# Sparse attention and a soft mixture of experts on one core: the order of all engine queues planned anew, with other prices

## The chip, the cores and the metric

The kernel runs on one core of one Trainium2 chip. The core has five engines that work side by side and each take their instructions in the order in which they were written: the matrix engine (PE in the profile, its weight loads PEld), VectorE (DVE), ScalarE (ACT), GpSimd (POOL) and SyncE (SP, which here only starts transfers). The metric is the device time of one execution in microseconds; the median of several executions is given.

## The reference

Eight batches of eight heads, 576 positions, head size 64. Attention keeps only those scores that lie within tau (0.02) of the row's largest. Its output, 4608 rows of 512, goes through a soft mixture of eight experts with four slots each.

```python
scores = scale * np.matmul(q, k.transpose(0, 1, 3, 2))
thresh = np.max(scores, axis=-1, keepdims=True) - tau
scores = np.where(scores >= thresh, scores, -1000000000.0)
attn = np.exp(scores - np.max(scores, axis=-1, keepdims=True))
attn = attn / (np.sum(attn, axis=-1, keepdims=True) + 1e-09)
x = np.matmul(attn, v)            # then laid out as (4608, 512)

logits = x @ phi                  # (4608, 32)
d = softmax of logits over the rows, c = softmax over the 32 slots
slot_input = d.T @ x
h = np.maximum(slot_input[e] @ w1[e], 0.0)     # for each expert e
slot_out[e] = h @ w2[e]
out = c @ slot_out
```

All is float32.

## The kernel before

Two heads of one batch make a pair; there are 32 pairs. A pair's 2 x 576 rows of scores are cut into nine blocks of 128 rows, eight of one head each and the ninth (the remainder) of both. For a block i:

- PE computes the scores (qk, L504; L509 for the ninth) into one of four regions of PSUM, each of two banks.
- DVE takes the largest of each row. In blocks 0, 2, 4, 6 and 8 it is a plain reduction (L522, nmx) and the scores stay in PSUM. In blocks 1, 3, 5 and 7 (the list AWAY) one instruction copies the negated scores to SBUF and takes the extreme on the way (L518, ss), so that the region is free at once.
- ACT computes the exponentials (L531, p, or pL for the ninth block). POOL makes the threshold from the maximum (L534, thr, one column).
- DVE compares the scores with the threshold, zeroes what lies below and sums the row, in one instruction (L538). In the AWAY blocks both its tensor inputs, ss and p, are in SBUF; in the others one is in PSUM.

After each second block POOL adds 1e-9 to the sums (L545, ri), DVE takes reciprocals (L548), POOL multiplies the two blocks by them (L552, p times ri, 128 x 576 each), PE transposes the scaled blocks (L429, ptr) and ACT copies them back to SBUF (L434, pTa, pTb, pTl). When all nine are there, PE multiplies by the values (L599), ACT copies the result (xT), PE transposes it again and ACT stores it (x). POOL also scales each pair's keys by 1/8 (L484). SP loads keys, queries and values (L477, L482, L489), two buffers of each.

After each fourth pair (one batch) the function dispatch adds the router's logits and the running sums of the dispatch softmax. Behind the last pair come the experts and the combination (from L894 on); that tail is written by hand and isn't planned. Its weights are loaded during attention, into buffers and into space that attention has given back.

The order of everything up to the tail comes from a planner, the class Order. Functions such as pair and dispatch hand each step to Order.add with an engine, a duration in ns, a nominal place, and the buffers that it reads and writes. Order.plan then plays the program through: whenever an engine is free, it takes from its ready steps the one with the lowest nominal place whose buffers are free. A step becomes ready when those before it have ended and a latency has passed: SAME for a step behind another of its own engine, LAT for one behind another engine's. The starts that come out sort the instructions into the engines' queues. On the chip each engine then follows its queue and waits where an input isn't there.

The nominal place of a step is its pair's base (nine steps a pair) plus a number of the table TABLE. There are tables for the first pair, the last, those between ("pair", 90 numbers, used by pairs 1 to 30), for the dispatch of an even, an odd and the last batch, and for the softmax over the slots ("soft"). A lower number goes first.

Buffers that set what can run ahead: four PSUM regions, four buffers p2 for two blocks of exponentials each, four of nmx and of thr, two of ss (SLOTS).

Of the kernel before, what the change touches and what calls it, by code (L numbers as in the profile page):

```python
# [17 lines left out]
LAT = {"PE": 197, "DVE": 140, "ACT": 152, "POOL": 160, "SP": 4500}  # L18
# [18 lines left out]
for _n, _v in (  # L37
    ("first", [
# [7 lines left out]
    ]),  # L46
    ("pair", [
# [7 lines left out]
    ]),  # L55
    ("last", [
# [7 lines left out]
    ]),  # L64
    ("even", [
        11.70, 6.26, 20.27, 11.43, 9.24, 4.36, 12.47, 23.16, 21.02, 7.45, 12.14, -0.83, -28.24, 0.76,
        8.10, -112.07, -111.39, 12.77, 9.31, 51.37, 18.87,
    ]),
    ("odd", [
        15.17, 39.73, 8.52, 14.62, 8.10, 2.55, 9.85, 14.30, 12.02, -15.66, 1.70, 14.42, 66.80, -1.30,  # L70
        10.34, 27.16, 5.02, -5.68, 21.85, 41.74, 36.19, -19.82, -3.87,
    ]),
    ("end", [
# [3 lines left out]
    ]),  # L77
    ("soft", [
        26.07, 93.95, 64.32, 18.60, -8.26, 26.88,
    ]),  # L80
):
    TABLE.update({(_n, _i): _x for _i, _x in enumerate(_v) if _x is not None})
# [19 lines left out]
class Order:  # L102
# [3 lines left out]
    def __init__(self, slots):  # L106
        self.slots = {k: list(v) for k, v in slots.items()}
        self.ops = []
        self.noms = []
        self.seen = set()  # L110
        self.newest = {}
        self.where = ["", 0, 0]
        self.writers = {}
        self.readers = {}
# [14 lines left out]
    def add(self, eng, dur, nom, fn, r=(), w=(), after=(), mode=HALVES):  # L129
        i = len(self.ops)  # L130
        name, base, n = self.where
        self.where[2] += 1
        self.noms.append((name, n, base, nom - base))
        r = [self.key(x) for x in r]
        w = [self.key(x) for x in w]
        deps = set(after)
        for x in r:
            deps.update(self.hits(self.writers, x))
        for x in w:
            deps.update(self.hits(self.writers, x))  # L140
            deps.update(self.hits(self.readers, x))
        for x in r:
            self.readers.setdefault(x[0], {}).setdefault(x[1], []).append(i)
        for x in w:
            self.writers.setdefault(x[0], {}).setdefault(x[1], []).append(i)
        bufs = {id(x[0]): x[0] for x in r + w}.values()
        for x in bufs:
            if x not in self.seen:
                self.seen.add(x)
                self.newest[x.kind] = i  # L150
        self.ops.append((eng, dur, fn, sorted(deps), list(bufs), mode))

    def plan(self, table):
# [46 lines left out]
        mode = None  # L200
        ev = [(0.0, 1, i) for i in range(n) if left[i] == 0]
        heapq.heapify(ev)
        while ev:
# [10 lines left out]
            for eng in engs:  # L214
# [21 lines left out]
                end = t + o[1]  # L236
                if eng == "PE":
                    end += SWITCH * (o[5] != mode)
                    mode = o[5]
                engfree[eng] = end  # L240
                heapq.heappush(ev, (end, 2, -1))
                heapq.heappush(ev, (end + LAT[eng], 0, got))
                for j in succ[got]:
                    left[j] -= 1
                    lat = (SAME if ops[j][0] == eng else LAT)[eng]
# [25 lines left out]
def softmax_attention_soft_moe(  # L271
# [170 lines left out]
    def dve(dur, nom, r, w, fn):  # L442
        G.add("DVE", dur, nom, fn, r, w)
# [13 lines left out]
    def pair(p):  # L457
# [38 lines left out]
        for i in range(N9):  # L496
# [4 lines left out]
            def qk(i=i, c=c, h=h, s=s):  # L501
                for g in range(2):
# [9 lines left out]
            G.add("PE", 540 if i < 8 else 486, t + OFF['qk'], qk, [kt[h], qt[h, 0], qt[h, 1]] if i < 8 else [kt, qt], [s],  # L512
                  mode=HALVES if i < 8 else QUADS)
            away = i in AWAY
            ss = Buf("ss") if away else s
            if away:

                dve(729, t + OFF['mx'], [s], [ss, nmx], lambda s=s, ss=ss, nmx=nmx: nc.vector.tensor_scalar(  # L518
# [8 lines left out]
            else:  # L527
# [3 lines left out]
            G.add("ACT", 624, t + OFF['ex'], lambda sv=sv, nmx=nmx, view=view, away=away: nc.scalar.activation(  # L531
# [5 lines left out]
            dve(950 if away else 729, t + OFF['st'], [ss, thr], [dst, r[i]],  # L537
                lambda sv=sv, thr=thr, view=view, i=i, away=away: nc.vector.scalar_tensor_tensor(  # L538
# [4 lines left out]
            if h == 1 or i == 8:  # L543
                e = slice(i // 2 * 2, i + 1)
                pool(200, t + OFF['ri'], lambda e=e: nc.gpsimd.tensor_scalar(  # L545
# [523 lines left out]
```

## Time and profile before

| | us |
|---|---|
| median of 3 runs | 597.59 |
| lowest and highest | 593.55 and 598.43 |
| span of the profiled execution | 595.4 |

The profile is of one execution. Its pages give busy time by engine, busy time by stretch, groups of instructions by line (count, busy us, mean ns of one, idle time of the engine just before them and who ended it), who waited for whom, and the instructions in order of time. A busy PE isn't PE at its peak, since matmuls overlap and their ends are modelled. An engine's idle time counts only where that engine bounds the work.

### The profile page before, as it was taken

To read this page: it belongs to the slowest core of one execution; us is meant where nothing else is said; L and a number is where in the kernel's file an instruction comes from. 1 tells how busy PE (TensorE), PEld (TensorE's weight loads), DVE (VectorE), ACT (ScalarE), POOL (GpSimd) and SP (SyncE) were. 2 spreads that over 40 slices of the span, in tenths; PEclk is the share of its full clock that TensorE was granted. 3 is DMA by queue.
4 is the path that set the end of the run, shared out by engine and by line. 5 is a ranking of instruction groups with operands and counts; after the bars stand their busy time and mean duration, and the time that the engine had idled before them with its cause. 6 is when DMAs were issued, how large, how long until landed. Compare 5 with 4: busy or idle time off the path is not lost. (4 is left out here: it accounts for less than half of the span.)

```text
span 595.4 us, 17443 instructions
## 1 busy us (share of the span) xinstructions
PE 548.3 (92%) x6404; PEld 340.6 (57%) x6404; DVE 496.8 (83%) x1275; ACT 448.2 (75%) x753; POOL 410.8 (69%) x799
## 2 busy tenths in 40 slices
PE   8799999999999999999999999999999899799991
PEld 6465665555665565566666655556666465453471
DVE  5889998999999989999999999999999889231183
ACT  3588887988888888888888978898888778422071
POOL 2778886888878887888788868887888666411030
PEclk9699999999999999999999999999999989899996
DMA  6245554455445555333333333333333312799678
GB/s 167 61 94 148 160 154 137 138 147 155 129 133 158 150 154 149 83 84 84 83 85 83 85 83 83 84 83 84 84 83 84 83 32 67 245 367 407 253 306 328
DMA packets 31988, 82.97 MB, mean 139 GB/s; under 512 B 4640, under 2 KB 12832, under 8 KB 31904
## 3 DMA queue, kind: packets, MB, share of 16 engines
q1 hardware_dynamic: 31904, 81.87, 46.8%
q8 instruction: 50, 0.82, 0.6%
q14 instruction: 34, 0.28, 0.2%
HBM read 72.42 MB, written 9.44 MB: 137 GB/s over the span
## 5 line engine op out<-in xcount | busy, mean ns | idle before, releaser
L552 POOL TENSOR_SCALAR p<-p,ri 128x576 f32<-128x576 f32 x256 | 206.8, 815 | 27.2 <-DVE ri L548 11.3
L504 PE MATMUL ps<-k,q 64*128 64x288 f32 x1024 | 170.1, 437 | 16.8 <-DVE ss L518 11.3
L429 PEld LDWEIGHTS ps<-ident,p 64*128 64x128 f32 x2304 | 92.2, 140 | 59.8 <-POOL p L552 17.8
L538 DVE SCALAR_TENSOR_TENSOR p<-ss,thr,p 128x576 f32<-128x576 f32 x128 | 116.9, 915 | 4.4 <-POOL thr L534 2.9
L522 DVE TENSOR_REDUCE nmx<-ps 128x1 f32<-128x576 f32 x160 | 116.8, 752 | 4.3 <-PE ps L504 2.9
L429 PE MATMUL ps<-ident,p 64*128 64x64 f32 x2304 | 108.9, 228 | 10.0 <-POOL p L552 6.1
L504 PEld LDWEIGHTS ps<-k,q 64*128 64x128 f32 x1024 | 85.9, 190 | 51.0 <-DVE ss L518 18.7
L538 DVE SCALAR_TENSOR_TENSOR p<-ps,thr,p 128x576 f32<-128x576 f32 x128 | 101.9, 811 | 8.9 <-POOL thr L534 7.3
L531 ACT ACTIVATE p<-ss,nmx 128x576 f32<-128x576 f32 x128 | 96.7, 776 | 12.8 <-DVE ss L518 12.4
L518 DVE TENSOR_SCALAR_CACHE_REDUCE ss<-ps 128x576 f32<-128x576 f32 x128 | 96.0, 750 | 6.7 <-PE ps L504 5.4
L434 ACT COPY pTb<-ps 128x1024 f32<-128x1024 f32 (+1 forms) x95 | 82.1, 874 | 21.0 <-PE ps L429 19.2
L531 ACT ACTIVATE p<-ps,nmx 128x576 f32<-128x576 f32 x128 | 91.9, 739 | 6.4 <-DVE nmx L522 3.9
L534 POOL TENSOR_SCALAR thr<-nmx,nabs 128x1 f32<-128x1 f32 x160 | 70.6, 445 | 11.2 <-DVE nmx L522 6.3
L599 PE MATMUL ps<-pTb,vv 128*64 128x320 f32 x512 | 76.0, 439 | 1.9 <-ACT pTb L434 1.7
L434 ACT COPY pTa<-ps 128x1024 f32<-128x1024 f32 x64 | 64.8, 1012 | 11.5 <-PE ps L429 8.6
L545 POOL TENSOR_SCALAR ri<-r 128x2 f32<-128x2 f32 (+1 forms) x160 | 38.9, 243 | 48.4 <-DVE p L538 21.0
L599 PE MATMUL ps<-pTa,vv 128*64 128x256 f32 x512 | 65.5, 400 | 0.0
L599 PEld LDWEIGHTS ps<-pTb,vv 128*64 128x64 f32 x512 | 33.9, 136 | 30.7 <-ACT pTl L434 2.2
L534 POOL TENSOR_SCALAR thr<-nmx,pabs 128x1 f32<-128x1 f32 x128 | 36.6, 286 | 15.8 <-DVE ss L518 10.9
L599 PEld LDWEIGHTS ps<-pTa,vv 128*64 128x64 f32 x512 | 35.2, 142 | 18.1 <-issue 2.2
L599 PE MATMUL ps<-pTl,vv 128*64 128x256 f32 (+1 forms) x256 | 41.9, 406 | 0.0
L859 POOL TENSOR_TENSOR c<-lall,crow 128x512 f32<-128x512 f32 x9 | 9.3, 1043 | 43.9 <-PE ct L421 38.9
(133 smaller groups left out, 605.4 us busy)
## 6 DMA issues: line engine op xcount, KB each, us to landing
w<-in_w SPq DMA_DIRECT2D x44, 512.0 KB, 6.7
q<-in_qT SPq DMA_DIRECT2D x62, 288.0 KB, 4.6
vv<-in_vt SPq DMA_DIRECT2D x32, 320.0 KB, 3.1
host<-in_w SPq DMA_DIRECT2D x20, 512.0 KB, 6.1
k<-in_kT SPq DMA_DIRECT2D x62, 144.0 KB, 4.9
out<-w SPq DMA_DIRECT2D x8, 512.0 KB, 3.3
out<-host SPq DMA_DIRECT2D x8, 512.0 KB, 5.0
out<-host SPq DMA_DIRECT2D x4, 256.0 KB, 4.4
```

Source lines behind the costliest of these rows:

```text
L429: nc.tensor.transpose(out=s[:, g, c:c + 64], in_=ins[g], identity=ident[rows[g], rows[g]], tile_position=(64 * g, 0))
L434: G.add("ACT", 51 + 0.833 * n, nom, lambda: nc.scalar.copy(*io()), r, w)
L504: nc.tensor.matmul(s.t[:, g, 0:HS], qt.t[rows[g], h, c * 128:(c + 1) * 128], kt.t[rows[g], h * HS:(h + 1) * HS], start=True, stop=True, ti ...
L518: dve(729, t + OFF['mx'], [s], [ss, nmx], lambda s=s, ss=ss, nmx=nmx: nc.vector.tensor_scalar(out=ss.t.rearrange("p (a k) -> p a k", a=2), ...
L522: dve(665, t + OFF['mx'], [s], [nmx], lambda s=s, nmx=nmx: nc.vector.tensor_reduce(out=nmx.t, in_=s.t[:, :, 0:HS], axis=AX.XY, op=ALU.max, ...
L531: G.add("ACT", 624, t + OFF['ex'], lambda sv=sv, nmx=nmx, view=view, away=away: nc.scalar.activation(view().rearrange("p (a k) -> p a k", ...
L534: pool(250, t + OFF['th'], lambda nmx=nmx, thr=thr, away=away: nc.gpsimd.tensor_scalar(out=thr.t, in0=nmx.t, scalar1=1.0 if away else -1.0 ...
L538: lambda sv=sv, thr=thr, view=view, i=i, away=away: nc.vector.scalar_tensor_tensor(out=view().rearrange("p (a k) -> p a k", a=2), in0=sv() ...
L545: pool(200, t + OFF['ri'], lambda e=e: nc.gpsimd.tensor_scalar(out=ri.t[:, e], in0=r.t[:, e], scalar1=1e-9, scalar2=1.0, op0=ALU.add, op1= ...
L552: pool(725, t + OFF['sc'], lambda k=k, view=view_: nc.gpsimd.tensor_scalar(out=view(), in0=view(), scalar1=ri.t[:, k:k + 1], **one), [ri[c ...
L599: nc.tensor.matmul(lone(w)[h * 64:(h + 1) * 64, 0:n], vv.t[:, v0:v0 + 64], p0, start=(kb == 0), stop=(kb == 4), tile_position=(0, h * 64), ...
L859: nc.gpsimd.tensor_tensor(out=c4, in0=lall[:, rows].unsqueeze(2).to_broadcast([128, k, 4, NS]), in1=crow[:, rows].unsqueeze(2).unsqueeze(3 ...
```

## The change

No step is added or taken out. Three things change in the planner and its inputs.

First, its prices. LAT is changed, and a new table CROSS gives a latency for seven pairs of engines. Several durations are changed: scores, the copy of the AWAY blocks, the exponential, the threshold sums, and the small step before the reciprocal. Scores get another 120 ns of latency (more=120). A PE step that starts after PE has been idle costs 50 ns more.

Second, a rule for DVE and POOL. The threshold sums of the AWAY blocks carry port=True. Where POOL is still at work when such a sum starts, the sum is made longer by 0.4 of what is left of POOL's step; and a POOL step that starts while such a sum runs is made longer by what is left of the sum.

Third, all seven tables are replaced. In "pair", the numbers of DVE's steps go from between -55 and +81 to between -365 and -206, those of ACT from between -76 and +30 to between -197 and -106. POOL's thresholds go from between -48 and +62 to between -124 and -59, its scalings of blocks 0, 1 and 8 from +31, +21 and +15 to +121, +122 and +122, the other scalings from between -34 and +42 to between -92 and -44. PE's go from between -74 and +12 to between -7 and +17. For SP the keys go from -3.06 to +10.31, the queries from -29.12 and -61.01 to +21.95 and +20.10, the values from +30.02 to +25.05. In "even" and "odd" many numbers go from between -112 and +67 to several hundred below zero, the lowest to -1092.31. Steps of other kinds (weight loads, warm-up) keep their places.

```diff
-LAT = {"PE": 197, "DVE": 140, "ACT": 152, "POOL": 160, "SP": 4500}
+LAT = {"PE": 252, "DVE": 150, "ACT": 165, "POOL": 86, "SP": 4500}
+CROSS = {("PE", "DVE"): 260, ("DVE", "ACT"): 182, ("DVE", "POOL"): 220, ("ACT", "DVE"): 237, ("ACT", "POOL"): 250,
+         ("POOL", "DVE"): 61, ("POOL", "ACT"): 100}
 SAME = {"PE": 0, "DVE": 127, "ACT": 143, "POOL": 0, "SP": 2100}
...
     ("even", [
-        11.70, 6.26, 20.27, 11.43, 9.24, 4.36, 12.47, 23.16, 21.02, 7.45, 12.14, -0.83, -28.24, 0.76,
-        8.10, -112.07, -111.39, 12.77, 9.31, 51.37, 18.87,
+        20.61, 146.84, 13.21, 163.00, 29.27, 166.25, 11.28, -584.76, -641.03, -307.50, 19.64, -567.09, -633.13, 123.48,
+        -13.49, -641.02, 163.01, -9.38, -650.04, -12.77, -683.63,
     ]),
...
-    def add(self, eng, dur, nom, fn, r=(), w=(), after=(), mode=HALVES):
+    def skip(self, n):
+        self.where[2] += n
+
+    def add(self, eng, dur, nom, fn, r=(), w=(), after=(), mode=HALVES, more=0, port=False, own=None):
...
-        self.ops.append((eng, dur, fn, sorted(deps), list(bufs), mode))
+        self.ops.append((eng, dur, fn, sorted(deps), list(bufs), mode, more, port))
...
                 end = t + o[1]
+                if o[7]:
+                    end += 0.4 * max(0.0, min(engfree["POOL"] - t, o[1]))
+                    held = end
+                if eng == "POOL" and held > t:
+                    end += held - t
                 if eng == "PE":
-                    end += SWITCH * (o[5] != mode)
+                    end += SWITCH * (o[5] != mode) + 50 * (engfree[eng] < t)
                     mode = o[5]
                 engfree[eng] = end
                 heapq.heappush(ev, (end, 2, -1))
-                heapq.heappush(ev, (end + LAT[eng], 0, got))
+                heapq.heappush(ev, (end + LAT[eng] + o[6], 0, got))
                 for j in succ[got]:
                     left[j] -= 1
-                    lat = (SAME if ops[j][0] == eng else LAT)[eng]
+                    lat = SAME[eng] if ops[j][0] == eng else CROSS.get((eng, ops[j][0]), LAT[eng]) + o[6]
...
-            G.add("PE", 540 if i < 8 else 486, t + OFF['qk'], qk, [kt[h], qt[h, 0], qt[h, 1]] if i < 8 else [kt, qt], [s],
-                  mode=HALVES if i < 8 else QUADS)
+            G.add("PE", 488 if i < 8 else 500, t + OFF['qk'], qk, [kt[h], qt[h, 0], qt[h, 1]] if i < 8 else [kt, qt], [s],
+                  mode=HALVES if i < 8 else QUADS, more=120)
...
-                dve(729, t + OFF['mx'], [s], [ss, nmx], lambda s=s, ss=ss, nmx=nmx: nc.vector.tensor_scalar(
+                dve(674, t + OFF['mx'], [s], [ss, nmx], lambda s=s, ss=ss, nmx=nmx: nc.vector.tensor_scalar(
...
-            G.add("ACT", 624, t + OFF['ex'], lambda sv=sv, nmx=nmx, view=view, away=away: nc.scalar.activation(
+            G.add("ACT", 668 if away else 630, t + OFF['ex'], lambda sv=sv, nmx=nmx, view=view, away=away: nc.scalar.activation(
...
-            dve(950 if away else 729, t + OFF['st'], [ss, thr], [dst, r[i]],
-                lambda sv=sv, thr=thr, view=view, i=i, away=away: nc.vector.scalar_tensor_tensor(
+            G.add("DVE", 738, t + OFF['st'], port=away, r=[ss, thr], w=[dst, r[i]],
+                fn=lambda sv=sv, thr=thr, view=view, i=i, away=away: nc.vector.scalar_tensor_tensor(
...
-                pool(200, t + OFF['ri'], lambda e=e: nc.gpsimd.tensor_scalar(
+                pool(292, t + OFF['ri'], lambda e=e: nc.gpsimd.tensor_scalar(
```

More of the change, by code (lines that the diff above doesn't have):

```diff
@@ L38 @@
     ("first", [
[7 rows of a table removed]
[7 rows of a table added]
     ]),
     ("pair", [
[7 rows of a table removed]
[7 rows of a table added]
     ]),
     ("last", [
[7 rows of a table removed]
[7 rows of a table added]
     ]),
     ("even", [
-        11.70, 6.26, 20.27, 11.43, 9.24, 4.36, 12.47, 23.16, 21.02, 7.45, 12.14, -0.83, -28.24, 0.76,
-        8.10, -112.07, -111.39, 12.77, 9.31, 51.37, 18.87,
+        20.61, 146.84, 13.21, 163.00, 29.27, 166.25, 11.28, -584.76, -641.03, -307.50, 19.64, -567.09, -633.13, 123.48,
+        -13.49, -641.02, 163.01, -9.38, -650.04, -12.77, -683.63,
     ]),
     ("odd", [
-        15.17, 39.73, 8.52, 14.62, 8.10, 2.55, 9.85, 14.30, 12.02, -15.66, 1.70, 14.42, 66.80, -1.30,
-        10.34, 27.16, 5.02, -5.68, 21.85, 41.74, 36.19, -19.82, -3.87,
+        16.01, -65.21, 13.21, -81.20, 26.13, -98.85, 7.02, -280.60, -256.65, -1092.31, 18.10, -183.06, -214.95, -85.79,
+        -4.28, -274.17, -81.33, -258.17, -63.02, 23.32, -252.02, -7.84, -187.13,
     ]),
     ("end", [
[3 rows of a table removed]
[3 rows of a table added]
     ]),
     ("soft", [
-        26.07, 93.95, 64.32, 18.60, -8.26, 26.88,
+        6.88, 35.49, -71.51, 6.87, 39.48, 49.38,
     ]),
@@ L112, in __init__ @@
         self.where = ["", 0, 0]
+        self.own = {}
         self.writers = {}
@@ L127, in scope @@
         self.where = [name, base, 0]
-    def add(self, eng, dur, nom, fn, r=(), w=(), after=(), mode=HALVES):
+    def skip(self, n):
+        self.where[2] += n
+    def add(self, eng, dur, nom, fn, r=(), w=(), after=(), mode=HALVES, more=0, port=False, own=None):
         i = len(self.ops)
-        name, base, n = self.where
-        self.where[2] += 1
+        where = self.where if own is None else self.own.setdefault((own, self.where[1]), [own, self.where[1], 0])
+        name, base, n = where
+        where[2] += 1
         self.noms.append((name, n, base, nom - base))
@@ L200, in plan @@
         mode = None
+        held = 0.0
         ev = [(0.0, 1, i) for i in range(n) if left[i] == 0]
```

48 rows, old and new, of the table TABLE are left out of this document.

## The prediction

> **What bounds the kernel now.** I read the page's busy times first.
>
> ```profile
> span 595.4 us, 17443 instructions
> PE 548.3 (92%) x6404; PEld 340.6 (57%) x6404; DVE 496.8 (83%) x1275; ACT 448.2 (75%) x753; POOL 410.8 (69%) x799
> ```
>
> No engine is full, so I cut the span into stages with the view of busy time by stretch (columns: sum of the stretch, then busy time and count of PE, PEld, DVE, ACT, POOL, granted clock, DMA share, GB/s).
>
> ```profile
> 0.00:30.00 30.00, 24.49 (x162) 16.53 (x162) 20.28 (x58) 13.02 (x18) 15.44 (x44) 0.83 0.48 113
> 30.00:480.00 450.00, 427.99 (x5342) 268.79 (x5340) 421.58 (x1094) 384.60 (x644) 362.60 (x703) 1.00 0.42 111
> 480.00:531.60 51.60, 45.20 (x538) 28.34 (x534) 33.66 (x92) 32.09 (x57) 25.46 (x47) 0.97 0.49 171
> 531.60:595.40 63.80, 50.64 (x373) 26.91 (x372) 21.27 (x33) 18.52 (x34) 7.26 (x7) 0.92 0.84 329
> ```
>
> The change can act on the first 531.6 us; the last 63.8 us are written after the planned part and stay. In the 450 us of steady attention PE is idle 22.0 us and DVE 28.4 us: two engines, each nearly full, take turns in waiting for each other. POOL has 87.4 us to spare there and bounds nothing by itself.
>
> The step from pair to pair comes from one row per pair, the threshold sum of the remainder block, in the view in order of time:
>
> ```profile
> 210.04 0.82 DVE L538 SCALAR_TENSOR_TENSOR pL<-ps,thr,pL 128x576 f32<-128x576 f32 x1
> 318.85 0.82 DVE L538 SCALAR_TENSOR_TENSOR pL<-ps,thr,pL 128x576 f32<-128x576 f32 x1
> 333.51 0.82 DVE L538 SCALAR_TENSOR_TENSOR pL<-ps,thr,pL 128x576 f32<-128x576 f32 x1
> ```
>
> Eight pairs with their two dispatches take 123.47 us, 15.4 us a pair; one pair without a dispatch takes 14.66 us.
>
> Then the groups by line (count, busy us, mean ns, idle time before and what ended it):
>
> ```profile
> L538 DVE SCALAR_TENSOR_TENSOR p<-ss,thr,p 128x576 f32<-128x576 f32 x128 | 116.9, 915 | 4.4 <-POOL thr L534 2.9 <-ACT p L531 1.1
> L538 DVE SCALAR_TENSOR_TENSOR p<-ps,thr,p 128x576 f32<-128x576 f32 x128 | 101.9, 811 | 8.9 <-POOL thr L534 7.3 <-ACT p L531 1.0
> L534 POOL TENSOR_SCALAR thr<-nmx,nabs 128x1 f32<-128x1 f32 x160 | 70.6, 445 | 11.2 <-DVE nmx L522 6.3 <-DVE ri L548 1.4 <-DMA k<-in_kT 0.2
> L534 POOL TENSOR_SCALAR thr<-nmx,pabs 128x1 f32<-128x1 f32 x128 | 36.6, 286 | 15.8 <-DVE ss L518 10.9 <-DVE crow L772 2.4 <-DVE ri L548 1.7
> L552 POOL TENSOR_SCALAR p<-p,ri 128x576 f32<-128x576 f32 x256 | 206.8, 815 | 27.2 <-DVE ri L548 11.3 <-PE ps L509 4.9 <-PE ps L504 3.2
> ```
>
> The same sum over the same 576 columns takes 915 ns with both inputs in SBUF and 811 ns with one in PSUM. The same one-column threshold takes 445 ns in one group and 286 ns in the other. Why, one place in order of time shows:
>
> ```profile
> 123.22 0.74 POOL L484 TENSOR_SCALAR k<-k,flag 128x576 f32<-128x576 f32 x1
> 123.45 1.11 DVE L538 SCALAR_TENSOR_TENSOR p<-ss,thr,p 128x576 f32<-128x576 f32 x1
> 123.94 1.23 POOL L552 TENSOR_SCALAR p<-p,ri 128x576 f32<-128x576 f32 x1
> ```
>
> The sum starts 0.51 us before POOL's key scaling ends and takes 1.11 us, 0.30 more than 811 ns. The next POOL instruction starts inside the sum and takes 1.23 us, where the scaling before it took 0.74. Each holds the other up, and the later one pays. The Trainium skill, page "SBUF — State Buffer", section "Who interferes with whom", says that a DVE instruction with two SBUF inputs contends with a GpSimd instruction that reads SBUF, and that the one issued second fully blocks until the first finishes. Here that would make the sum 0.51 + 0.81 = 1.32 us; the row has 1.11, so most of the instruction is blocked, not all of it.
>
> Last, who waited for whom (us, times, longest):
>
> ```profile
> DVE ri L548 <- POOL ri L545: 8.9, 22, 2.0
> PE ps L504 <- DVE ss L518: 11.3, 20, 1.2
> PEld ps L429 <- POOL p L552: 17.8, 26, 1.4
> PE ps L429 <- POOL p L552: 6.1, 17, 1.1
> POOL k L484 <- DMA k<-in_kT: 3.8, 5, 2.3
> SPq L489 <- PE ps L599: 345.4, 30, 17.6
> ```
>
> **The change part by part.** No instruction is added, removed or resized: 17443 before and after, apart from waits. All that moves is the order in each engine's queue, through the planner's prices and the priority table.
>
> *The prices come nearer to the trace.* Three links, each where the later engine stood waiting:
>
> ```profile
> 222.45 0.74 PE L504 MATMUL ps<-k,q 64*128 64x288 f32 x4
> 223.31 0.76 DVE L522 TENSOR_REDUCE nmx<-ps 128x1 f32<-128x576 f32 x1 [0.24 <-PE ps L504]
> 98.95 1.42 DVE L522 TENSOR_REDUCE nmx<-ps 128x1 f32<-128x576 f32 x2 [0.26 <-PE ps L504]
> 99.81 0.27 POOL L534 TENSOR_SCALAR thr<-nmx,nabs 128x1 f32<-128x1 f32 x1 [0.20 <-DVE nmx L522]
> 153.38 0.76 ACT L531 ACTIVATE p<-ps,nmx 128x576 f32<-128x576 f32 x1
> 154.24 0.82 DVE L538 SCALAR_TENSOR_TENSOR p<-ps,thr,p 128x576 f32<-128x576 f32 x1 [0.32 <-ACT p L531]
> ```
>
> From start to start, scores to maximum is 0.86 us (the old plan reckons 540 + 197 = 0.74, the new one 488 + 120 + 260 = 0.87), maximum to threshold 0.86 (old 665 + 140 = 0.81, new 0.89), exponential to sum 0.86 (old 624 + 152 = 0.78, new 630 + 237 = 0.87). The old plan put work 0.05 to 0.12 us too early at each of these links in every one of nine blocks a pair, and so let other work be queued behind an instruction that was not ready. On the other side it gave a two-SBUF sum a flat 950 ns, while its own row means 915, and nothing to POOL for being held.
>
> *DVE's stretch.* 128 x (915 - 811) = 13.3 us, all on an engine that is idle only 6% of the steady stage. The new plan lets a sum that starts while POOL is at work pay 0.4 of what is left, so a start beside a wide POOL instruction now has a price, though a low one: 0.4 x 0.51 = 0.20 where the row shows 0.30. POOL is busy 81% of the stage, so most sums will still meet it. Between nothing and all, I take half: 6.6 us. By the skill's full block the same place would cost 0.51; a plan that asks 0.20 for it would then be 2.5 times too cheap to keep sums clear of POOL, and with nothing of the stretch recovered the time would be 591.2 us.
>
> *DVE waiting for POOL's small results.* 2.9 + 7.3 us for thresholds and 8.9 us for reciprocals, 19.1 us. A threshold is late where it was held behind a sum or queued behind a scaling of 815 ns. In the new table of a pair the thresholds stand between -124 and -59, most scalings between -92 and -44, and those of blocks 0, 1 and 8 at +121 and +122, so small work more often overtakes wide work. But some of what goes here turns into DVE waiting for PE. I take a third: 6.4 us. Ends: 19.1 gained, or 6.4 lost if the holds fall worse.
>
> *PE's waits for a PSUM region* (11.3 us for scores behind the copy that empties one) depend on DVE getting to that copy. PE's and DVE's waits are two sides of one loop, so I count nothing for them beyond the two terms above. Uncovered it is 11.3 us either way.
>
> *The dispatch of a batch* goes from table values near 0 to values as low as -1092, ahead of everything. It costs DVE the same instructions; what it displaces waits once per batch, eight times at most one 815 ns instruction, 6.5 us, if nothing is queued to cover it; I take 0, since every attention block has neighbours ready.
>
> *The loads on SP.* In the table of a pair, keys go from -3 to +10 and queries from -61 and -29 to +20 and +22, still before the values at +25. Against them the weight loads, with no table, now come first when both are ready. Cover: SP sits 345.4 us waiting for a value buffer, so it is early by far. If the cover goes, the nearest price is POOL's 3.8 us of waiting for keys. I take 0, ends -3.8 and +3.8.
>
> *The last pair and the end of attention* (480 to 531.6): PE is idle 6.4 us there, DVE 17.9. Its tables are drawn anew, with no reason in the rows for a sign: 0, ends -6 and +6.
>
> Sum: 6.6 + 6.4 = 13.0 us, so a span of 582.4. The profiled execution's span is 2.2 us under the 597.59 us median of the runs; with that kept, **584.6 us**, 2.2% faster. A difference over 1% (6 us) is about what a measurement of this kernel can tell from no change.
>
> **The rivals.**
> *Larger gain.* All of stretch and POOL waits goes, 13.3 + 19.1 = 32.4 us. PE's own idle time caps it: 22.0 + 6.4 = 28.4 us, so 597.6 - 28.4 = 569.2. For it: every price moved towards the rows. Against: POOL has to fit 363 us of work beside DVE's sums whatever the order.
>
> *No change.* PE is 95% busy in the steady stage, and what DVE saves comes back as PE waiting for regions and scalings: about 595 to 598. For it: 11.3 us of score blocks waiting for a region, and no buffer is added. Against: the stretch of 13.3 us is real DVE work that a mere shift between waits doesn't restore. The skill's page "Perfetto Trace Analysis", section "Optimization Strategy", says that the same gap repeated on the engine that should be saturated can mean too little SBUF or PSUM for the next tile; by that an order alone would leave these gaps, and the four regions stay four.
>
> *Slower.* The scalings of blocks 0 and 1 go to the very end of POOL's priorities (+121 and +122, from +31 and +21), and the transposes of that pair of blocks need both. PE already waits 17.8 us before weight loads and 6.1 us before matmuls for scalings. One more wide POOL instruction of 815 ns in front in each of 31 pairs, exposed on PE, costs 25.3 us: 597.6 - 13.0 + 25.3 = 609.9. It decides from 16 exposed ones on, every second pair. Against: four buffers for pairs of blocks stand between, and POOL is idle a fifth of the stage.
>
> **How the numbers follow.** Chances: the forecast, from 577 to 591.6, 0.50; larger gain, below 577, 0.12; no change within 1%, 0.23; slower, 0.15. So faster 0.62, same 0.23, slower 0.15. The range may leave out 0.2: it runs from the larger gain's 569 to 602, which leaves out the slower cases (0.15) and the top of "no change", with the losing ends above (6.4, 3.8 and 6 us) set one at a time against half the gain. The forecast's own range is 577 to 592.
>
> **What would show it.** Right: the mean of the two-SBUF sum falls from 915 towards 860, DVE's idle time for thresholds and reciprocals from 19.1 to about 13, the plain step from 14.66 to about 14.2, PE busier than 95% in the stage. Wrong: the stretch stays and POOL's wide instructions are held as before; or DVE's waits shrink while rows of PE waiting for the scalings at L552 or for L518 grow by as much; or keys come late on POOL.

## The result, and the profile after

| | us |
|---|---|
| before, median of 4 runs (593.55 to 598.43) | 596.94 |
| after, median of 4 runs (575.45 to 577.45) | 576.77 |
| ratio, with its 95% interval | 0.968 (0.964 to 0.971) |
| span of the profiled execution, before and after | 595.4 and 574.5 |

The changed kernel is 3.2% faster; 2.2% was forecast, 584.6 us with a range of 569 to 602. The page after (line numbers have moved by 13: L517 is the scores, L531 the copy to ss, L535 the maximum, L547 the threshold, L551 the sums, L558 and L561 the reciprocal's two steps, L565 the scaling):

```profile
span 574.5 us, 17496 instructions
PE 537.0 (93%) x6404; PEld 334.3 (58%) x6404; DVE 489.8 (85%) x1275; ACT 442.2 (77%) x753; POOL 398.1 (69%) x799
```

The same work in the same number of instructions on each engine; only waits were added. Busy time by stretch after the change:

```profile
0.00:30.00 30.00, 24.45 (x216) 17.15 (x216) 21.69 (x63) 15.44 (x24) 16.19 (x47) 0.94 0.47 114
30.00:460.00 430.00, 415.16 (x5258) 261.51 (x5256) 409.70 (x1078) 374.60 (x636) 346.11 (x693) 1.00 0.42 115
460.00:509.10 49.10, 45.78 (x565) 29.25 (x560) 37.17 (x103) 33.64 (x60) 28.41 (x53) 1.00 0.49 172
509.10:574.50 65.40, 51.59 (x372) 26.39 (x372) 21.28 (x33) 18.52 (x34) 7.42 (x8) 0.92 0.84 331
```

PE is now busy 96.5% of the steady stage, from 95.1%, and 93% of the end, from 88%. To say where the time went I cut both kernels at the same events, the remainder sums (pL) of pairs 1 and 29 and the first expert matmul, in the view in order of time, before and then after:

```profile
41.53 0.81 DVE L538 SCALAR_TENSOR_TENSOR pL<-ps,thr,pL 128x576 f32<-128x576 f32 x1
473.76 0.81 DVE L538 SCALAR_TENSOR_TENSOR pL<-ps,thr,pL 128x576 f32<-128x576 f32 x1
531.58 0.64 PE L894 MATMUL h<-w,siT 128*32 128x512 f32 x4
```

```profile
38.08 0.81 DVE L551 SCALAR_TENSOR_TENSOR pL<-ps,thr,pL 128x576 f32<-128x576 f32 x1
293.25 0.81 DVE L551 SCALAR_TENSOR_TENSOR pL<-ps,thr,pL 128x576 f32<-128x576 f32 x1
307.50 0.81 DVE L551 SCALAR_TENSOR_TENSOR pL<-ps,thr,pL 128x576 f32<-128x576 f32 x1
458.90 0.81 DVE L551 SCALAR_TENSOR_TENSOR pL<-ps,thr,pL 128x576 f32<-128x576 f32 x1
509.13 1.05 PE L907 MATMUL h<-w,siT 128*32 128x512 f32 x6
```

| stretch | before | after | gained |
|---|---|---|---|
| start to pair 1 | 41.5 | 38.1 | 3.4 |
| pair 1 to pair 29 | 432.2 | 420.8 | 11.4 |
| pair 29 to the first expert matmul | 57.8 | 50.2 | 7.6 |
| tail | 63.8 | 65.4 | -1.6 |

The step between two pairs without a dispatch falls from 14.66 us to 14.25 (307.50 - 293.25). The groups after:

```profile
L551 DVE SCALAR_TENSOR_TENSOR p<-ss,thr,p 128x576 f32<-128x576 f32 x128 | 110.2, 873 | 1.0
L551 DVE SCALAR_TENSOR_TENSOR p<-ps,thr,p 128x576 f32<-128x576 f32 x128 | 103.8, 812 | 2.5 <-POOL thr L547 0.3 <-issue 0.2
L561 DVE RECIPROCAL ri<-ri 128x2 f32<-128x2 f32 (+1 forms) x160 | 22.9, 156 | 1.0 <-POOL ri L558 0.9
L565 POOL TENSOR_SCALAR p<-p,ri 128x576 f32<-128x576 f32 x256 | 193.9, 762 | 12.0 <-DVE ri L561 3.1 <-PE ps L517 1.2 <-PE ps L442 0.7
```

The sums with both inputs in SBUF fell from 915 to 873 ns and POOL's scalings from 815 to 762. Who waited for whom between pair 1 and pair 29, before and after (us, times, longest):

```profile
DVE p L538 <- POOL thr L534: 9.0, 50, 0.4
DVE ri L548 <- POOL ri L545: 6.2, 19, 0.8
DVE ss L518 <- PE ps L504: 1.9, 6, 0.4
DVE nmx L522 <- PE ps L504: 1.0, 4, 0.3
PE ps L504 <- DVE ss L518: 9.9, 18, 0.6
PE ps L429 <- POOL p L552: 4.0, 15, 0.6
```

```profile
DVE p L551 <- POOL thr L547: 0.3, 1, 0.3
DVE ss L531 <- PE ps L517: 3.5, 13, 0.5
DVE nmx L535 <- PE ps L517: 6.9, 28, 0.3
PE ps L517 <- DVE ss L531: 5.1, 15, 0.3
```

DVE's waiting for POOL, 15.2 us, is all but gone. Its waiting for PE's scores grew from 2.9 to 10.4 us in its place: PE, 96.5% busy, now comes nearest to setting the pace of the steady stage.

Of the 11.4 us between pair 1 and pair 29, 7.4 are in the fifteen steps without a dispatch (221.2 us in all before, 213.8 after) and 4.0 in the thirteen with one (211.0 and 207.0). The gains at the start and at the end hold a part that belongs to the clock (last section).

### The profile page after: what moved, and what is told of

Its sections match the earlier page's. It is cut to its first block, busy times and chain, and to the rows that moved or that the text cites. A ratio compares the mean times of both kernels' runs of the same rounds, so it can differ in the third digit from the quotient of the medians.

```text
span 574.5 us, 17496 instructions
## 1 busy us (share of the span) xinstructions
PE 537.0 (93%) x6404; PEld 334.3 (58%) x6404; DVE 489.8 (85%) x1275; ACT 442.2 (77%) x753; POOL 398.1 (69%) x799
## 4 chain that ended last, share of the span: by engine, by line
PE 54%; DVE 15%; ACT 9%; issue 8%; POOL 8%; DMA 4%; SPq 1%; DVEq 0%; ACTq 0%; POOLq 0%
PE ps L612 23%; PE ps L442 11%; PE ps L517 11%; POOL p L565 4%; DVE p L551 4%; ACT pTb L447 4%; DVE ss L531 3%; DMA host<-in_w 3%; DVE nmx L535 3%; PE ps L522 2%; PE so L941 2%; POOL thr L547 2%; ACT pTl L597 2%; ACT pTl L447 2%; PE h L907 1%
## 5 line engine op out<-in xcount | busy, mean ns | idle before, releaser
L565 POOL TENSOR_SCALAR p<-p,ri 128x576 f32<-128x576 f32 x256 | 193.9, 762 | 12.0 <-DVE ri L561 3.1
L517 PE MATMUL ps<-k,q 64*128 64x288 f32 x1024 | 167.3, 431 | 8.4 <-DVE ss L531 6.5
L535 DVE TENSOR_REDUCE nmx<-ps 128x1 f32<-128x576 f32 x160 | 119.9, 753 | 11.7 <-PE ps L517 7.8
L551 DVE SCALAR_TENSOR_TENSOR p<-ss,thr,p 128x576 f32<-128x576 f32 x128 | 110.2, 873 | 1.0
L517 PEld LDWEIGHTS ps<-k,q 64*128 64x128 f32 x1024 | 85.2, 188 | 38.8 <-DVE ss L531 11.7
L551 DVE SCALAR_TENSOR_TENSOR p<-ps,thr,p 128x576 f32<-128x576 f32 x128 | 103.8, 812 | 2.5 <-POOL thr L547 0.3
L544 ACT ACTIVATE p<-ss,nmx 128x576 f32<-128x576 f32 x128 | 99.4, 781 | 8.2 <-DVE ss L531 8.1
L531 DVE TENSOR_SCALAR_CACHE_REDUCE ss<-ps 128x576 f32<-128x576 f32 x128 | 96.2, 752 | 7.5 <-PE ps L517 6.5
L544 ACT ACTIVATE p<-ps,nmx 128x576 f32<-128x576 f32 x128 | 94.5, 739 | 5.8 <-DVE nmx L535 4.1
L558 POOL TENSOR_SCALAR ri<-r 128x2 f32<-128x2 f32 (+1 forms) x160 | 43.9, 274 | 55.1 <-DVE p L551 36.0
L547 POOL TENSOR_SCALAR thr<-nmx,nabs 128x1 f32<-128x1 f32 x160 | 58.6, 367 | 21.2 <-DVE ri L561 13.4
L612 PE MATMUL ps<-pTa,vv 128*64 128x256 f32 x512 | 62.3, 385 | 0.6 <-DVE ss L531 0.4
L547 POOL TENSOR_SCALAR thr<-nmx,pabs 128x1 f32<-128x1 f32 x128 | 46.8, 366 | 12.3 <-DVE ss L531 8.4
```

The costliest lines, as they stand in the source:

```text
L517: nc.tensor.matmul(s.t[:, g, 0:HS], qt.t[rows[g], h, c * 128:(c + 1) * 128], kt.t[rows[g], h * HS:(h + 1) * HS], start=True, stop=True, ti ...
L531: dve(674, t + OFF['mx'], [s], [ss, nmx], lambda s=s, ss=ss, nmx=nmx: nc.vector.tensor_scalar(out=ss.t.rearrange("p (a k) -> p a k", a=2), ...
L535: dve(665, t + OFF['mx'], [s], [nmx], lambda s=s, nmx=nmx: nc.vector.tensor_reduce(out=nmx.t, in_=s.t[:, :, 0:HS], axis=AX.XY, op=ALU.max, ...
L544: G.add("ACT", 668 if away else 630, t + OFF['ex'], lambda sv=sv, nmx=nmx, view=view, away=away: nc.scalar.activation(view().rearrange("p ...
L547: pool(250, t + OFF['th'], lambda nmx=nmx, thr=thr, away=away: nc.gpsimd.tensor_scalar(out=thr.t, in0=nmx.t, scalar1=1.0 if away else -1.0 ...
L551: fn=lambda sv=sv, thr=thr, view=view, i=i, away=away: nc.vector.scalar_tensor_tensor(out=view().rearrange("p (a k) -> p a k", a=2), in0=sv(),
```

## The experiments

**GpSimd out of the way, in both orders.** If the gain came from how DVE and POOL meet, the old order should win most of it when POOL's scaling costs next to nothing, and the new one little. Two edits, each in both kernels with their queues unchanged: the scaling over one column, or a fill that writes as much and reads nothing. Both leave out the division by the row sums.

```diff
-    out=view(), in0=view(), scalar1=ri.t[:, k:k + 1], **one), [ri[c]], [dst_])
+    out=view()[:, 0:1], in0=view()[:, 0:1], scalar1=ri.t[:, k:k + 1], **one), [ri[c]], [dst_])
```

```diff
-    nc.gpsimd.tensor_scalar(out=view(), in0=view(), scalar1=ri.t[:, k:k + 1], **one)
+    nc.gpsimd.memset(view(), 1.0)
```

> The kernel before, queues unchanged, with GpSimd's scaling of the exponentials cut from 576 columns to 1 (the other 575 stay unscaled, so the attention output is not divided by its row sums). Theory A (the gain of the change comes from how VectorE and GpSimd meet: stretched sums, thresholds and reciprocals that come late): this order loses most of that, 13 to 25 us, and comes to 572 to 584. Theory B (the gain comes from all other prices: work queued behind something that was not ready on PE, ACT and DVE): GpSimd was not what held it, and it gains at most 6 us, 591 to 597.

> The changed kernel with the same cut: GpSimd's scaling over 1 column, the rest unscaled. Theory A: this order had already got rid of most meetings, so it gains less than the kernel before does, 3 to 10 us (567 to 574), and the distance between the two orders falls from 20 us to 12 or less. Theory B: the two gain alike, and the distance stays at 17 us or more.

> The kernel before with GpSimd's scaling replaced by a fill with ones of the same 128 x 576 (the exponentials are overwritten, so the attention weights are all one). GpSimd stays about as busy but reads nothing from SBUF for it. If the stretch of VectorE's two-SBUF sums comes from GpSimd's reads, their mean falls from 915 ns to about 815 and the fill isn't held; theory A with the port alone then gives 8 to 15 us (582 to 589). If GpSimd's being late is what counts, rather than the port, it gains under 4 us.

> The changed kernel with the same fill in place of the scaling. Theory A with the port alone: the sums fall from 873 ns to about 815, and the time by 3 to 8 us (569 to 574), less than in the kernel before. Otherwise the two move alike.

| | old order | new order | distance |
|---|---|---|---|
| as they are (the new one from the first comparison) | 596.6 | 576.8 | 19.8 |
| scaling of one column | 587.5 | 575.8 | 11.7 |
| fill | 588.5 | 576.3 | 12.2 |

The old order gains 9.1 and 8.1 us, the new one 1.0 and 0.5. Neither theory's numbers were met whole. A had asked for 13 us or more from the narrow scaling, B for 6 or less; with the fill the old order met A's 8 to 15, at 588.5, while the new order moved less than the 3 to 8 expected. The distance met A's 12 or less with the narrow scaling. POOL holds 8 of the 20 us, and 12 come from elsewhere. In the steady stage its share is 4 of the 11.4 us: from pair 1 to pair 29 the old order takes 427.7 and 427.9 us with the two edits in place of 432.2, the new one 420.6 and 420.5 in place of 420.8. The 7 us that stay between the orders are about as much in steps with a dispatch (210.8 and 206.9 with the narrow scaling) as in those without (217.0 and 213.7). The group of two-SBUF sums in the new order with the fill:

```profile
L551 DVE SCALAR_TENSOR_TENSOR p<-ss,thr,p 128x576 f32<-128x576 f32 x128 | 103.2, 812 | 5.2 <-ACT p L544 4.3
```

The fill keeps POOL at work on as many columns (577 ns a time, where the scaling took 762) and the sums are down to 812 ns from 873 (in the old order to 830 from 915), so it is POOL's reading that stretches them. (The Trainium skill, page "SBUF — State Buffer", section "Who interferes with whom", says that such a DVE instruction contends with a GpSimd instruction that reads SBUF and not with one that only writes it. The trace agrees.) And in the new order the stretch was harmless where it was left: 60 ns less on each sum changed the time by 1 us at most. The plain step, old order with narrow scaling and then new with it:

```profile
301.05 0.81 DVE L538 SCALAR_TENSOR_TENSOR pL<-ps,thr,pL 128x576 f32<-128x576 f32 x1
315.52 0.81 DVE L538 SCALAR_TENSOR_TENSOR pL<-ps,thr,pL 128x576 f32<-128x576 f32 x1
```

```profile
292.43 0.81 DVE L551 SCALAR_TENSOR_TENSOR pL<-ps,thr,pL 128x576 f32<-128x576 f32 x1
306.69 0.81 DVE L551 SCALAR_TENSOR_TENSOR pL<-ps,thr,pL 128x576 f32<-128x576 f32 x1
```

14.47 us and 14.26: in these rows 0.19 of the 0.41 us that the plain step gained is POOL and 0.22 is not.

**The other half of the step: one group of transposes.** PE's queues of the two orders, read from the traces, differ in a plain step mainly in one place: the transposes of blocks 0 and 1 stand before the previous pair's second product with the values in the old order, and behind that pair's last transposes in the new one. (The queues of DVE, ACT and POOL differ in more places.) What they run into, PE in order of time, old and new:

```profile
303.01 0.65 PE L429 MATMUL ps<-ident,p 64*128 64x64 f32 x16
304.31 1.25 PE L504 MATMUL ps<-k,q 64*128 64x288 f32 x6 [0.64 <-DVE ss L518]
```

```profile
292.35 0.71 PE L442 MATMUL ps<-ident,p 64*128 64x64 f32 x16
293.39 0.76 PE L517 MATMUL ps<-k,q 64*128 64x288 f32 x4 [0.33 <-DVE ss L531]
```

I gave the old plan that one constraint (with the old prices and table), then also the place of the copy that follows, then both with the narrow scaling.

```diff
-    def ptr(n, nom, r, w, triples):
+    def ptr(n, nom, r, w, triples, after=()):
...
-        G.add("PE", 62 * n, nom, fn, r, w)
+        G.add("PE", 62 * n, nom, fn, r, w, after)
...
-                    for h in range(2) for k in range(4)])
+                    for h in range(2) for k in range(4)],
+                    [xtr[-1]] if c == 0 and p % 4 > 1 and 1 < p < NP - 1 else [])
...
         w = Buf("s")
+        xtr.append(len(G.ops))
         ptr(4, u + OFF['x'], [xT], [w, x["t", j]], lambda w=w: [
```

> The kernel before with its prices and table, and one more constraint in its plan: in pairs p with p mod 4 of 2 or 3 the transposes of blocks 0 and 1 come behind the last transposes (x) of pair p - 1, where the changed kernel has them, in place of before that pair's second product with the values. Theory C (with GpSimd out of the way the step without a dispatch still was 14.47 us in the old order and 14.24 in the new; the rest is this move, which fills PE's wait of 0.64 us for a PSUM region): PE's wait before the third block's scores falls to about 0.35 us, and the step between two such pairs from 14.66 to 14.3 to 14.45, 3 to 5 us over all (592 to 594). Theory D (no single move pays; the parts of an order fit each other only as a whole): the step stays at 14.6 or grows, and the time is 596 or more.

Measured 602.7 us, ratio 1.012 (1.007 to 1.016): slower, theory D. The steps between two moved pairs take 14.73 to 15.47 us. PE's wait only moved, one group ahead:

```profile
303.57 0.71 PE L429 MATMUL ps<-ident,p 64*128 64x64 f32 x16 [0.72 <-ACT pTa L434]
```

These transposes wait for ACT's copy of the moved ones, which the old order places behind the remainder block's exponential. So the copy was moved too:

```diff
-                [ss, nmx], [dst])
+                [ss, nmx], [dst], pt0 if i == 8 and p % 4 > 1 and 1 < p < NP - 1 else [])
...
+                if c == 0:
+                    pt0[:] = [len(G.ops)]
                 act_copy(1024, t + OFF['te'], [w], [pT[c]], lambda c=c, w=w, pT=pT: (
```

> The move of the transposes of blocks 0 and 1 again, and with it the copy of their result on ScalarE ahead of the remainder block's exponential of the pair before, where the changed kernel has it (before, PE waited 0.72 us for that copy after the move). If the move failed for want of the copy in its place, the step between two moved pairs falls from 14.78 us with the move alone to 14.3 to 14.5, below the 14.66 of the kernel before, and the whole to 590 to 597; the steps with a dispatch are not planned for it and may stay longer. If the move pays only with the whole new order, that step stays at 14.7 or more.

> The same with GpSimd's scaling cut to 1 column (the rest unscaled). If the 0.42 us between the plain steps of the two orders (14.66 and 14.24) is GpSimd's part of 0.19 and this move's 0.23, nothing else is left and the step between two moved pairs comes to 14.2 to 14.3. If there is a third part it stays above 14.35.

With copy: 599.0 us, ratio 1.005 (1.003 to 1.007), still no gain. The seven steps between two moved pairs take 14.51 to 14.79 us and 14.67 on average, not the 14.3 to 14.5 expected. With the narrow scaling on top: 590.4 us, and the step is 14.29 where it was looked at (mean of the seven 14.39, the first two being longer):

```profile
300.77 0.81 DVE L540 SCALAR_TENSOR_TENSOR pL<-ps,thr,pL 128x576 f32<-128x576 f32 x1
315.06 0.81 DVE L540 SCALAR_TENSOR_TENSOR pL<-ps,thr,pL 128x576 f32<-128x576 f32 x1
```

Five of the seven steps are 14.25 to 14.30, as without a third part; the mean is above 14.35. So transposes and copy in the new places bring this one step of the old order to the new one's, but only with POOL out of the way. That they pay over the stage is not shown: the plain step behind it, into a pair that isn't moved, is 14.68 us where the narrow scaling alone has 14.47, and pair 1 to pair 29 takes 428.1 us against 427.7. With POOL at work they make its meetings worse. The group of sums with move and copy, POOL at full width:

```profile
L540 DVE SCALAR_TENSOR_TENSOR p<-ss,thr,p 128x576 f32<-128x576 f32 x128 | 121.1, 948 | 6.3 <-POOL thr L536 5.1 <-POOL ri L547 0.4 <-ACT p L533 0.3
```

The two halves aren't two independent edits, and no run here has the move and POOL's full work together at a gain. (The 590.4 us, 2.9 more than with the narrow scaling alone, include an end of 56.9 us in place of 53.8.)

**The prices alone.** All new prices and the rule, with the old table (the first lines of the edit, against the changed kernel).

```diff
-    ("first", [
-        -249.67, -228.94, -242.55, 86.26, -279.10, -285.18, -279.09, 21.49, -260.83, -14.00, 73.55, -89.27, -23.01, 140.75,
+    ("first", [
+        -91.66, -86.70, -91.31, -101.39, -117.22, -95.99, -92.60, -93.20, -71.14, -98.63, -93.39, -82.51, -117.60, -89.54,
...
```

> All new prices, with the rule for GpSimd, but the old table. If prices near the trace are what pays by themselves: 580 to 592. If table and prices are only worth something together, since the table's numbers were found for other prices: no gain or a loss, 597 to 630.

606.4 us, ratio 1.018 (1.014 to 1.022), slower. The meetings are there as before (906 ns for a two-SBUF sum), and DVE waits more for thresholds and exponentials:

```profile
DVE p L551 <- POOL thr L547: 12.4, 31, 0.9
DVE p L551 <- ACT p L544: 12.0, 25, 0.8
```

A price doesn't order anything by itself; a planner that takes the ready step of lowest number avoids a costly start only if the numbers were found under that price. The reverse, the new table under the old prices, was not run.

**The tables of the edges.** The old kernel with the new tables last, end and soft; and the new kernel with the old tables first, last, end and soft. The diffs exchange those lists and nothing else, such as

```diff
     ("soft", [
-        26.07, 93.95, 64.32, 18.60, -8.26, 26.88,
+        6.88, 35.49, -71.51, 6.87, 39.48, 49.38,
     ]),
```

in the first and the other way in the second.

> The kernel before with the tables last, end and soft of the changed kernel; pairs 0 to 30 keep their order nearly to the end. From the remainder sum of pair 29 to the first expert matmul the kernel before takes 57.8 us and the changed one 50.2. If the new tables of the end carry this by themselves: 51 to 54 us, and 4 to 6 us less in all (591 to 593). If they need the new prices and the new middle: 57 or more, 596 to 602.

> The changed kernel with the old tables first, last, end and soft. The steady stage should keep its step of 14.24 us. If start and end are worth what the two traces differ there (3.4 and 7.6 us): 584 to 590. If the tables of the edges matter little beside the prices: 577 to 580.

The first: 594.4 us, ratio 0.997 (0.995 to 0.999), and from pair 29's sum to the first expert matmul 54.6 us in place of 57.8 (527.71 - 473.09):

```profile
473.09 0.81 DVE L538 SCALAR_TENSOR_TENSOR pL<-ps,thr,pL 128x576 f32<-128x576 f32 x1
527.71 0.64 PE L894 MATMUL h<-w,siT 128*32 128x512 f32 x4
```

That is 3.2 of the 7.6 us, just short of what was expected if the tables carried it. The second: 596.3 us, ratio 1.000 (0.998 to 1.003), worse than the 584 to 590 expected. Its steady steps are the new kernel's, but the start and the end lose all that these win: the remainder sums of pairs 1 and 2 are 21.1 us apart, and the end takes 58.7 us (526.59 - 467.88).

```profile
35.03 0.82 DVE L551 SCALAR_TENSOR_TENSOR pL<-ps,thr,pL 128x576 f32<-128x576 f32 x1
56.14 0.81 DVE L551 SCALAR_TENSOR_TENSOR pL<-ps,thr,pL 128x576 f32<-128x576 f32 x1
467.88 0.81 DVE L551 SCALAR_TENSOR_TENSOR pL<-ps,thr,pL 128x576 f32<-128x576 f32 x1
526.59 0.64 PE L907 MATMUL h<-w,siT 128*32 128x512 f32 x4
```

**The rule for GpSimd.** Two tables found by the same random search, from the old table on, with the new prices and as many trials: one with the rule, one without it. All seven tables are other numbers in each, and in the second the rule is off:

```diff
-                if o[7]:
+                if False:
                     end += 0.4 * max(0.0, min(engfree["POOL"] - t, o[1]))
                     held = end
```

> New prices and the rule for GpSimd, with a table found by a random search that began at the old table and had the planner's own end as its aim (195,000 to 199,000 trials, the better of two). If prices together with a table found for them are what pays, it comes near the changed kernel: 577 to 585. If the changed kernel's table has something else, it stays near the kernel before, 590 or more.

> The same search with the same number of trials, without the rule for GpSimd (a two-SBUF sum costs nothing extra, GpSimd is never held in the plan), all other new prices kept. If the rule is a main part of the gain, this order meets GpSimd as often as the kernel before: two-SBUF sums at 900 ns or more, VectorE waiting 10 us or more for thresholds, and a time 5 us or more above the search with the rule. If the other prices carry the gain, it is within 1% of it, 577 to 587.

With the rule 584.1 us, ratio 0.980 (0.977 to 0.984), within the range expected. Without it 622.7 us, ratio 1.045 (1.041 to 1.048), 38.6 us apart. The rule makes the difference between these two tables, though not in the way that I had expected. With the rule, then without:

```profile
L551 DVE SCALAR_TENSOR_TENSOR p<-ss,thr,p 128x576 f32<-128x576 f32 x128 | 111.0, 880 | 3.4 <-ACT p L544 1.7 <-POOL thr L547 1.3
DVE ri L561 <- POOL ri L558: 2.7, 4, 2.2
PE ps L442 <- POOL p L565: 1.2, 2, 0.7
```

```profile
L551 DVE SCALAR_TENSOR_TENSOR p<-ss,thr,p 128x576 f32<-128x576 f32 x128 | 108.9, 857 | 4.4 <-ACT p L544 2.3 <-POOL thr L547 1.4 <-POOL p L565 0.3
DVE ri L561 <- POOL ri L558: 18.6, 39, 1.3
PE ps L442 <- POOL p L565: 19.0, 37, 1.0
```

The sums without the rule are no longer, 857 ns, and DVE waits 4.1 us for thresholds, 5.4 with the rule. What is late is POOL's other work: DVE waited 18.6 us for the step before the reciprocal and PE 19.0 us for scalings. POOL wasn't held more than with the rule, for it was busy 402.8 us here and 404.1 there. The likely reason is that the plan without the rule reckoned on POOL's steps ending sooner than they did, and put work behind them that was then not ready; no plan's own times are on record to show it. The stretch of the sum, which I had taken for the cost, isn't what separates the two. It is one table of each kind that ran, so the size of the 38.6 us is loose, and a better or worse find of the search may have a part in it; where the time goes is in the rows.

## Why the prediction was right

*The number.* 576.8 us is inside the range, but just under the forecast's own 577 to 591.6: it lies in the band of the larger gain, which was given 0.12. That rival's way, all of the stretch and of POOL's waits, didn't come, since 7.8 us of stretch are left. What came beyond the forecast is in the start and the end, where nothing had been put.

*The bound.* Two nearly full engines that wait for each other in turn, with POOL coming between: right. With POOL's wait gone DVE waits for PE, as the prediction's tests have it, and PE is above 95%.

*The stretch.* 6.6 us of 13.3 were forecast; 128 x (873 - 812) = 7.8 are left, so 5.5 went. The sum's term was near. As a saving in time it was not what it seemed: the new order kept 7.8 us of stretch at a cost of at most 1 us, as the fill showed.

*DVE waiting for POOL's small results.* I took a third of 19.1 us, 6.4. In fact nearly all went: over the whole span 0.3 us for thresholds and 0.9 for reciprocals are left of it, so 17.9 went (the remainder sums, which the term leaves out, wait 1.4 us in place of 0.4), and between pairs 1 and 29 7.5 us came back as waiting for PE. As waiting, this term was sized too low, and the reserve that some would turn into waiting for PE was right in kind. Thresholds overtaking scalings need not be all of it: the two searches suggest that POOL's held time had to be in the plan.

*PE's waits for a region* were set at nothing beyond those. The row fell from 9.9 to 5.1 us between the two pairs. Half of the plain step's gain, 0.22 us, is not POOL's; the moved transposes and their copy can give it in one step, which isn't shown for the whole stage. The rival "no change" leaned on the four regions staying four, and on the page "Perfetto Trace Analysis" of the Trainium skill, section "Optimization Strategy", by which repeated gaps can mean too little room. Here an order alone halved the gap in front of the third block's scores, 0.64 to 0.33 us, with no buffer more.

*The steady stage* together: 13.0 us forecast for all of it, 11.4 measured. The plain step was to fall to about 14.2 and is 14.25. That the sums come so near is in part luck. Both terms of the 13.0 us were meetings with POOL, and the two edits that take POOL out of the way give 4.5 and 4.3 us of the 11.4. Some 7 us came from what had been set at 0: the steps with a dispatch, and what isn't POOL's in the plain ones.

*Start and end* were set at 0, the end with ends of 6 us each way. They gained 3.4 and 7.6. This is where the forecast fell short by its 7 to 8 us: the last pair's tables were drawn anew and I saw no reason for a sign, though the rows showed PE idle 6.4 us there. About 2.5 us of the start and up to 3.4 of the end belong to the clock of the one execution before (below). What carries the end is shown only in part: its new tables alone gave 3.2 us, and the fill in the old order 5.1 (52.7 us in place of 57.8), both with a better clock.

*The dispatch and the loads*, set at 0. The thirteen steps with a dispatch gained 4.0 us, of which POOL out of the way gives the old order 0.3; no experiment changed the dispatch tables by themselves. POOL's waiting for keys fell from 3.8 to 2.2 us. The tail lost 1.6 us, and its rows show one wait that has grown, from 0.4 us:

```profile
PEld h L907 <- DMA host<-in_w: 2.1, 3, 1.1
```

The experts now start 22 us sooner, and PE waits three times for a weight tile that isn't there yet. I had not looked at what a faster attention collides with. The earlier start can't be all of the reason: with the move and the copy the experts start 3.5 us later than in the kernel before (535.09 us), and the same wait is 1.2 us there.

*The rivals.* The slower one, scalings of blocks 0 and 1 sorted last on POOL, did not come: between pairs 1 and 29 PE's 4.0 us of waiting for scalings went to nothing that the view lists. Its transposes were put later as well, so their lateness was planned.

## What to carry to other kernels

What a plan's prices leave out can cost more than the slow instruction that one sees: an engine that is held by another is late for everyone behind it, and the two searches, one table each, point that way. Change prices and order together, edges included; a new price under an old order, or a new middle between old edges, gave nothing or a loss here. And when a stage is planned anew, ask what the next one needs to have loaded by then. Before a gain in one stage is put down to the order, compare the granted clock there.

## What the runs showed of the hardware

A two-SBUF sum that starts while a wide POOL instruction has R left doesn't take R longer. In the kernel before, 58 sums between 60 and 480 us started inside a wide POOL instruction (from the start and end of each row in order of time); in 50 of them more than 0.25 us of it was left, and there the sum's time less R was 601 to 609 ns each time, 200 ns under the 813 that the 24 sums took that met no wide POOL instruction. So the rows look as if the first 0.2 us of a sum ran beside POOL and it then waited for POOL's end; that POOL gives way 0.2 us before its recorded end would give the same rows. The Trainium skill's page "SBUF — State Buffer", section "Summary: rules for kernel authors", has the second one fully blocked; the rows agree but for that 0.2 us. The plan's 0.4 R is neither, and still served.

The clock moved the start. With the same queues up to pair 1, the old order was there at 41.53, 40.93 and 38.95 us in three executions (the kernel before, the one with new tables at the end, the one with the transposes moved); their first 30 us, in the last two:

```profile
0.00:30.00 30.00, 24.66 (x176) 16.63 (x178) 19.92 (x58) 13.37 (x19) 15.05 (x43) 0.89 0.49 113
```

```profile
0.00:30.00 30.00, 24.92 (x212) 17.49 (x213) 21.57 (x60) 15.23 (x21) 16.22 (x45) 0.94 0.48 113
```

In the kernel before the granted clock is 0.50 all the way from 20 to 28 us and 1.00 before 18 us, so these means are stretches at half speed among full speed: 0.83, 0.89 and 0.94 are 10, 7 and 4 us of them (30 us times twice what is missing). The new order's 38.08 us came with 0.94. Like with like it gains 0.9 us at the start (38.95 less 38.08), and some 2.5 us of the 3.4 are the clock's.

The end has it too. From pair 29's sum to the first expert matmul the granted clock was 0.94 in the kernel before (3.4 us at 0.51 from 476.6 us on, and 3.4 at 0.50 from 510.7), 0.97 with the new tables of the end, and 1.00 in the changed kernel. By the same arithmetic 6.8 us at half speed can cost 3.4 us, so up to 3.4 of the 7.6 us gained there, and up to 1.7 of the 3.2 with the new tables, may be the clock's. Over whole executions it is the same: the kernel before had 0.976 to 0.991 in the 19 runs beside the moved transposes, and its one run at 0.989 took 592.9 us; the changed kernel had 0.985 to 0.989, and its two runs at 0.989 took 575.5 and 576.9. On these few runs the change is worth 16 to 17.5 us at a like clock, rather than 20. Whether the new order itself brings the better clock, no run here separates.
